# A new written order of all steps, and other engines for 93 of them, in a gated linear attention followed by a gated MLP

## The chip, the core and the metric

The kernel runs on one NeuronCore of a Trainium2 chip. The core has a matrix engine (TensorE, PE), a vector engine (VectorE, DVE), a scalar engine (ScalarE, ACT), a general engine (GpSimd, POOL) and a queue engine (SyncE, SP), each with its own list of instructions that it takes in order, and 16 DMA engines that move data between HBM and on-chip memory. The metric is the device time of one execution in microseconds (us); lower is better.

## What is computed

Two parts follow each other: a linear attention with a complex decay for each key channel, and a gated MLP with a gated residual.

```python
batch, n_heads, seq, head_dim = (4, 8, 768, 48)
mag = np.sqrt(a_re * a_re + a_im * a_im)
scale = np.minimum(mag, 0.999) / (mag + 1e-06)
a_re_n, a_im_n = (a_re * scale, a_im * scale)
for t in range(S):
    new_re = ar * S_re - ai * S_im
    new_im = ar * S_im + ai * S_re
    kv = np.einsum('bhd,bhe->bhde', k[:, :, t], v[:, :, t])
    S_re, S_im = (new_re + kv, new_im)
    y[:, :, t] = np.einsum('bhd,bhde->bhe', q[:, :, t], S_re)
...
g = x @ w_gate                      # x: 3072 x 384, w_gate and w_val: 384 x 1536
gelu = 0.5 * g * (1.0 + erf(g * inv_sqrt2))
val = x @ w_val
ffn_out = gelu * val @ w_out        # w_out: 1536 x 384
res_gate = 1.0 / (1.0 + np.exp(-(x @ w_res)))
return x + res_gate * ffn_out
```

x is the attention's output with the heads side by side: 4 x 768 tokens of 8 x 48 channels.

## The kernel before

**Tiling.** The sequence of each batch is cut into three stretches of 256 tokens. A stretch of a batch is a *pair* p, from 0 to 11: p = 4 s + b for stretch s and batch b. A pair has two *chunks* c of 128 tokens, on the 128 partitions. The recurrence becomes products of triangular matrices inside a chunk and a state of 48 x 48 (twice, for the real and imaginary part) handed from chunk to chunk and, by batch, from pair p to pair p + 4. The MLP works on *units* u of tokens: units 0 to 3 are pairs 0 to 3, units 4 to 7 are two pairs each (4 and 5, 6 and 7, and so on).

**Steps.** Every piece of work is a named step, added with its engine, its function, and what it reads and writes (class Steps, line 354). A step's name is letters, pair (or unit), and then chunk and half. By groups:

- Loads on SP, 192 KB each: Lar, Lai, Lq, Lk, Lvf with pair and chunk (lines 522 to 525 and 889). VC casts v to bf16.
- Gates of a pair (lines 527 to 668): SQI and SQR square the imaginary and real part, ADD adds them, LNR and EXR make the inverse of the magnitude or real part, TH the tangent, LM the logarithm, ATN the angle. CSL and CST are running sums over the tokens (fp32 products with a triangular matrix on PE). EX and EI are exponentials of the sums, in E and Ei. OFF and FR reduce the angle to one turn, ABS its size, SIN and COS the rotation (tile CS).
- State and carries: DR, DS, DI, DT, DE, CDA and CDB are small DMAs on POOL; ML, ME, MM and MN make the decay of the state; CRA and CRB scale a carried row; EN decays the state, EB copies it to bf16, MI and ED add to it.
- Products (lines 691 to 711): QE, KE, QR, KR scale and rotate q and k into padQ and padK. For pairs 0 to 4, TP transposes them on PE and CP evicts; from pair 5 on, QT and KT are transposing DMAs on SP.
- Attention (lines 713 to 808): AT makes scores, AM masks them, DK updates the state, Y makes the output, X casts it to bf16.
- Unit (lines 813 to 882): XT and XC transpose x on PE for pairs 0 to 4, XD is a transposing DMA on SP from pair 5 on. GP and VP are gate and value products, GE the gelu, HM the product of both, RP and SG the residual gate, OP the output product, OT its eviction with the gate, RX adds x, ST stores 192 KB on SP.
- Weights: Wg0 to Wg3 and Wv0 to Wv3 (a quarter each of w_gate and w_val, 288 KB), Wr, Wo0 to Wo2, as casting DMAs on POOL. HOLDW and HOLDO are one-element copies on POOL that read ai of pair 2, chunk 1, and ai of pair 4, chunk 1; POOL goes on when these loads have landed.

**Tables of ACT.** The words log, trig and gelu in the order load the function table for LNR, EXR, LM, EX, EI, ML and ME; for ATN, SIN and COS; and for GE and SG (line 938). Copies, squares and casts run with any.

**What sets the order.** Nothing is reordered at build time: the text ORDER (from line 268) lists all steps, and each engine takes its own steps in that order. The digits after a colon choose the buffers that the step's tiles take. PARAMS['eo'] (from line 64) names the engine of the steps that may go to one of several; without an entry a default holds. A step waits, in its engine's list, for the tiles that it reads and for the release of the buffers that it takes, and everything behind it on that engine waits too. The loop that runs it:

```python
for nm in ORDER(st) if callable(ORDER) else ORDER.split():
    if nm in tables:
        nc.scalar.preload_act_table_set(tables[nm])
    else:
        st.run(*nm.split(":"))
```

Of the kernel before, what the change touches and what calls it, by code (L numbers as in the profile page):

```python
# [79 lines left out]
        'CP4.0.0': 'ACT',  # L80
# [33 lines left out]
        'EN8': 'DVE',  # L114
# [69 lines left out]
        'SQI11': 'DVE',  # L184
        'SQI2': 'DVE',
# [3 lines left out]
        'SQI6': 'ACT',  # L189
# [3 lines left out]
        'SQR0.0': 'ACT',  # L193
        'SQR0.1': 'ACT',
        'SQR1': 'DVE',
        'SQR10': 'ACT',
        'SQR11': 'ACT',
        'SQR2': 'ACT',
# [32 lines left out]
        'X0.1': 'DVE',  # L231
        'X1.0': 'DVE',
        'X1.1': 'DVE',
        'X10.0': 'ACT',
        'X10.1': 'ACT',
        'X11.0': 'DVE',
# [12 lines left out]
        'X7.1': 'DVE',  # L249
        'X8.0': 'ACT',  # L250
        'X8.1': 'ACT',
        'X9.0': 'DVE',
        'X9.1': 'ACT',
        'XC0.0': 'DVE',
        'XC0.1': 'DVE',
        'XC1.0': 'DVE',
        'XC1.1': 'DVE',
        'XC2.0': 'DVE',
        'XC2.1': 'ACT',
        'XC3.0': 'DVE',  # L260
# [23 lines left out]
TH4 VP0.4:1 GE0.5 HM0.3 VP0.0:2 Lai7.1 HM0.4 VP0.1:0 X1.0 trig ATN2 VP0.2:3 HM0.0 XT1.0:11 SIN3:0 HM0.1 VP0.5:2 HM0.2
ATN4 Y1.1:3 CST2.1:0 Lq2.1:2 X1.1 ATN5 CDB0 XC1.0 XT1.1:3 OFF2.1 CST2.0:1 Lq2.0 XC1.1 DR5:1 HM0.5 RP0.0:3 OFF2.0 CDB1
FR2.1 Lq3.1:3 OP0.1.0:2 COS3 FR2.0 DE3:3 Lq3.0 ABS2 SIN2:1 VC2.1 KE2 Lar6.1:2 COS2 OP0.0.0:0 DS5.1:1 Lk3.1:3 OT0.1:0
CRB2 ED1 Lar7.0:1 KR2 GP1.2:1 gelu SG0.0 Lk3.0 GP1.3:2 OT0.0:1 GE1.2 QE2 GP1.0:3 SQI7:3 Lvf3.0:0 GP1.5:0 GE1.0 QR2
VP1.3:1 Lq6.0:1 GE1.5 QE3 TP2.0.1:30 GE1.3 VP1.0:0 CP2.0.1 Lai6.0:1 CSL4.0:211 HM1.3 AT2.0.1:00 log LM5 TP2.0.0:31
# [682 lines left out]
```

## Time and profile before

| | |
|---|---|
| runs | 273.61, 271.89, 273.48 us; median 273.48 |
| profiled execution, its own time | 271.4 us |
| its span, first to last instruction | 269.6 us |
| mean granted clock of TensorE | 0.958 of full |
| DMA | 41.35 MB moved, 153 GB/s in the mean |
| ACT table loads | 32 |

The profile is of one execution. Busy time is the time in which an engine worked at an instruction; a wait in front of an instruction is not busy. A matmul's end is modelled, so PE that shows as busy is not always at its peak rate. In the rows of 40 slices each digit is the busy share of one fortieth of the span in tenths; PEclk is the clock that TensorE was granted, in tenths. In the tables of stretches the columns are named in the head line. The DMA share is the mean busy share of the 16 DMA engines and goes over 1 where packets of several transfers overlap.

### The profile page before, as it was taken

What the parts mean: (1) busy time and instruction counts of PE and PEld (TensorE: products, weight loads), DVE (VectorE), ACT (ScalarE), POOL (GpSimd) and SP (SyncE); (2) the same over time, 40 slices, a digit from 0 to 9 for tenths busy, and PEclk for the clock granted to TensorE, in tenths of its full rate; (3) what the DMA queues carried; (4) which work ended last, traced back from release to release, by engine and by line L of the source; (5) the groups of instructions that cost most, each with busy time, mean ns of one, the idle gap of its engine ahead of it and who ended that gap; (6) DMA issues with size and microseconds to landing.
All of it is one profiled execution on the core that took longest, in us unless ns stands there. A gap on an engine that the chain in (4) does not pass through costs nothing. (4 is left out here: it accounts for less than half of the span.)

```text
span 269.6 us, 5323 instructions
## 1 busy us (share of the span) xinstructions
PE 235.4 (87%) x1926; PEld 147.7 (55%) x1926; DVE 220.9 (82%) x359; ACT 205.3 (76%) x334; POOL 113.6 (42%) x163
## 2 busy tenths in 40 slices
PE   0364778799998989899988999999999999999993
PEld 0121444586775677577844556645556455654451
DVE  0548898999999999999998998978889998733642
ACT  3779999999999999789996899987967843115310
POOL 4003338304436799347695177630853400040001
PEclk9998555999999999999999999999999999999998
DMA  7999999999996999999979969379942484021002
GB/s 147 212 209 210 220 173 186 200 186 191 197 175 139 160 178 166 238 208 174 175 140 229 238 140 183 73 142 244 139 64 72 121 202 123 21 77 65 2 29 88
DMA packets 170714, 41.35 MB, mean 153 GB/s; under 512 B 162624, under 2 KB 170688, under 8 KB 170688
## 3 DMA queue, kind: packets, MB, share of 16 engines
q1 hardware_dynamic: 163200, 37.04, 67.3%
q0 software_dynamic: 7488, 3.97, 11.4%
q8 instruction: 15, 0.25, 0.4%
q14 instruction: 11, 0.09, 0.1%
HBM read 31.33 MB, written 4.76 MB: 134 GB/s over the span
## 5 line engine op out<-in xcount | busy, mean ns | idle before, releaser
L509 ACT ACTIVATE h<-gv 128x512 bf16<-128x512 f32 x72 | 40.0, 598 | 27.4 <-PE gv L837 26.9
L848 DVE SCALAR_TENSOR_TENSOR h<-h,gv 128x512 bf16<-128x512 bf16 x72 | 46.9, 680 | 12.5 <-PE gv L837 8.4
L837 PE MATMUL gv<-xT,wv 128*128 128x256 bf16 (+1 forms) x288 | 54.8, 325 | 1.3 <-DVE ot L867 0.7
L837 PE MATMUL gv<-xT,wg 128*128 128x256 bf16 (+1 forms) x288 | 52.5, 326 | 1.9 <-DVE ot L867 0.7
L862 PE MATMUL sums<-wo,h 128*128 128x384 bf16 x288 | 49.2, 326 | 0.1
L938 ACT ACT_TABLE_LOAD x32 | 41.1, 1283 | 1.3 <-PEq L955 0.7
L874 POOL TENSOR_TENSOR ot<-ot,x 128x384 f32<-128x384 f32 x18 | 19.7, 1101 | 52.6 <-DVE ot L867 47.9
L837 PEld LDWEIGHTS <-wg 128*128 128x128 bf16 x288 | 27.4, 98 | 19.3 <-issue 3.2
L862 PEld LDWEIGHTS <-h 128*128 128x128 bf16 x288 | 27.5, 98 | 17.7 <-issue 0.4
L837 PEld LDWEIGHTS <-wv 128*128 128x128 bf16 x288 | 27.2, 98 | 18.0 <-issue 2.8
L751 DVE TENSOR_TENSOR atm<-at,mask 128x512 bf16<-128x512 f32 x48 | 32.5, 684 | 3.3 <-PE at L748 2.8
L509 ACT ACTIVATE ar<-ar 128x768 f32<-128x768 f32 (+1 forms) x33 | 26.8, 820 | 0.6 <-DVE m L573 0.5
L867 DVE SCALAR_TENSOR_TENSOR ot<-sg,sums 128x384 f32<-128x384 f32 x24 | 13.0, 549 | 11.5 <-PE sums L862 7.3
L631 PE MATMUL sums<-ai,ut 128*128 128x384 f32 x40 | 17.6, 532 | 5.2 <-issue 2.6
L520 POOL CAST v<-vf 128x384 bf16<-128x384 f32 x17 | 13.8, 815 | 17.2 <-DMA vf<-in_v_dram 15.5
L684 POOL DMA_DIRECT2D ai<-G x16 | 14.7, 939 | 14.7 <-ACT ai L509 12.2
L597 PE MATMUL sums<-m,ut 128*128 128x384 f32 x24 | 12.6, 629 | 8.5 <-ACT m L509 8.4
L573 DVE CUSTOM_DVE_ANT_0 m<-m,ar 128x768 f32<-128x768 f32 (+1 forms) x13 | 11.5, 889 | 6.3 <-ACT m L509 6.2
L509 ACT ACTIVATE sg<-sums 128x384 f32<-128x384 f32 x24 | 11.5, 492 | 5.3 <-PE sums L852 5.0
L852 PE MATMUL sums<-wr,xT 128*128 128x384 bf16 x72 | 14.8, 325 | 0.0
L605 POOL DMA_DIRECT2D d<-E x8 | 4.9, 616 | 23.3 <-ACT E L509 23.3
L611 POOL DMA_DIRECT2D m<-d x16 | 13.0, 837 | 3.8 <-DMA d<-Ei 3.7
(94 smaller groups left out, 463.0 us busy)
## 6 DMA issues: line engine op xcount, KB each, us to landing
ar<-in_a_re_dram SPq DMA_DIRECT2D x24, 192.0 KB, 3.8
k<-in_k_dram SPq DMA_DIRECT2D x24, 192.0 KB, 3.9
ai<-in_a_im_dram SPq DMA_DIRECT2D x24, 192.0 KB, 3.8
q<-in_q_dram SPq DMA_DIRECT2D x24, 192.0 KB, 3.7
vf<-in_v_dram SPq DMA_DIRECT2D x24, 192.0 KB, 3.8
out_dram<-ot SPq DMA_DIRECT2D x24, 192.0 KB, 2.0
wv<-in_moe_w_val_dram POOLq DMA_DIRECT2D x4, 288.0 KB, 6.9
wg<-in_moe_w_gate_dram POOLq DMA_DIRECT2D x4, 288.0 KB, 6.8
```

What stands on the lines that cost most here:

```text
L509: return nc.scalar.activation(out=out, in_=in_, func=func, **kw)
L520: return (nc.vector if eng == "DVE" else nc.gpsimd).tensor_copy(out=out, in_=in_)
L611: st.add("DT%d.%d" % (p, u), "POOL", lambda u=u: nc.gpsimd.dma_start(out=st["m3", p][u * D:(u + 1) * D].rearrange("p r h -> p (r h)"), in_ ...
L631: return r + [nc.tensor.matmul(out=o, lhsT=tmat[c if s == 0 else 1], rhs=part(("ai", p), (c,)), start=not both, stop=True)]
L684: st.add("CD%s%d" % (nm, p), "POOL", lambda: nc.gpsimd.dma_start(out=part(("ai", pn), (cn,))[0:1], in_=row[127:128], accum_op=OP.add), r=[ ...
L751: st.add("AM" + sfx, "DVE", lambda: nc.vector.tensor_tensor(out=st["atm", i], in0=st["at", i], in1=mask4, op=OP.mult), r=[("at", i)], w=[( ...
L837: st.add("%sP%d.%d" % (nm.upper(), u, f), "PE", lambda f=f, fs=fs, nm=nm, w=w: [nc.tensor.matmul(out=st[nm + "p", (u, f)][:, j * 256:j * 2 ...
L848: st.add("HM%d.%d" % (u, f), "DVE", lambda f=f, h2=h2: nc.vector.scalar_tensor_tensor(out=h2(), in0=h2(), scalar=0.5, in1=gv(("vp", (u, f) ...
L852: st.add("RP%d.%d" % (u, jj), "PE", lambda jj=jj: [nc.tensor.matmul(out=st["rp", (u, jj)], lhsT=st["xT", u][:, i, jj * 128:(jj + 1) * 128] ...
L862: st.add("OP%d.%d.%d" % (u, jj, hh), "PE", lambda jj=jj, fs=fs: [nc.tensor.matmul(out=st["op", (u, jj)], lhsT=st["h2", u][:, f, jj * 128:( ...
L874: st.add("RX%d.%d" % (u, jj), rese, lambda jj=jj, pc=(p, c), eng=eng: eng.tensor_tensor(out=st["ot", (u, jj)], in0=st["ot", (u, jj)], in1= ...
L938: nc.scalar.preload_act_table_set(tables[nm])
```

## The change

Only PARAMS['eo'] and ORDER differ. The set of steps is the same; the order has 11 log and 10 gelu switches in place of 12 and 11, and 9 trig as before. All buffer counts, units and functions stay.

Engines of 93 steps change. By kind, the number on each engine before and after:

| steps | before | after |
|---|---|---|
| X | ACT 14, DVE 10 | ACT 20, DVE 4 |
| XC | ACT 3, DVE 7 | ACT 4, DVE 6 |
| RX | POOL 18, DVE 6 | POOL 13, DVE 11 |
| SQR | ACT 11, DVE 2 | ACT 8, DVE 5 |
| SQI | ACT 7, DVE 6 | ACT 7, DVE 6 (four swap) |
| VC | ACT 4, DVE 3, POOL 17 | ACT 5, DVE 2, POOL 17 |
| CRA, CRB | ACT 6, DVE 2, POOL 8 | ACT 3, DVE 7, POOL 6 |
| EN, EB, MM, MN | ACT 2, DVE 10, POOL 20 | ACT 2, DVE 6, POOL 24 |
| CP, OFF | ACT 17, DVE 27 | ACT 17, DVE 27 (20 swap) |

Some entries, and the first lines of the order up to the first gate products:

```diff
-        'SQR0.0': 'ACT',
-        'SQR0.1': 'ACT',
+        'SQR0.0': 'DVE',
+        'SQR0.1': 'DVE',
...
-        'SQR2': 'ACT',
+        'SQR2': 'DVE',
...
-        'X0.1': 'DVE',
+        'X0.1': 'ACT',
...
-        'XC0.1': 'DVE',
+        'XC0.1': 'ACT',
...
-Lar0.1:0 Lk0.0:0 Lai0.0:0 Lai0.1 Lai1.1:1 log LNR0.1:0 Lar0.0 SQR0.1 Lai1.0 Lai5.1:2 SQI0.1:0 Lai3.1:3 ADD0.1 LM0.1
-Lar1.0:1 LNR0.0 Lai2.0:4 EXR0.0 CSL0.1:00 SQI1:1 SQI0.0 Lq1.0:0 SQR0.0 EXR0.1 ADD0.0 Lar1.1 TH0.1 TH0.0 Lk0.1 trig
-ATN0.1 ATN0.0 Lar3.1:2 CST0.1:1 Lvf0.0:0 OFF0.1 Lq0.0:1 SQR1 Lai2.1 ADD1 log LM0.0 Lar3.0 CSL0.0:2 FR0.1 LM1 Lar4.1:3
...
-LM3 Lar5.1:1 QE0.0 SQR4 MI0:0 Lq1.1 QR0.0 EX1.1 QR0.1 EI1.1 TP0.0.0:20 Lar5.0 DE1:1 EX1.0 OFF1.0 Wv3 TP0.0.1:31
-Lvf1.0:1 LNR3 FR1.0 Wg2 Lvf2.0:0 CSL3.1:100 ABS1 EXR3 SQI4:0 EI1.0 SQR2 KE1 EI3.1 CP0.0.0 CP0.0.1 AT0.0.0:00 ADD4
-AT0.0.1:11 trig COS1:1 TP0.1.1:00 DK0.1 TH3 TP0.1.0:21 CRB1 DR4:0 SIN1 CSL3.0:3 AM0.0.1 Wv1 ATN3 ADD2 Wg1 KR1 Wg3
-CP0.1.0 Wv2 log LNR2 AM0.0.0 Wg0 CP0.1.1 SQI5:1 Y0.0:0 Wr AT0.1.0:10 EX3.0 CST3.0:2 DS4.1:0 LM2 AM0.1.0 Wo0 QE1 SQR5
...
-OFF3.1 XC0.1 TP1.1.0:20 EX3.1 FR3.1 DS4.0 AT1.0.0:01 LM4 TP1.1.1:31 CRB3 VC1.0 XT0.0:1 EXR2 XC0.0 Lvf2.1:1 CP1.1.1
-GP0.0:0 CP1.1.0 Lai7.0:0 AM1.0.0 Lk2.1:2 GP0.3:1 AM1.0.1 GP0.2:3 ABS3 DK1.0 Y1.0:2 Lk2.0 gelu GE0.3 AT1.1.0:00 MI1:1
...
+Lai0.0:0 Lai1.1:1 Lar0.0:0 Lar0.1 Lar1.0:1 SQI0.0:0 Lar1.1 Lai0.1 log LNR0.0:0 Lai1.0 EXR0.0 SQR0.0 LNR0.1 Lar3.0:2
+EXR0.1 SQR0.1 ADD0.0 Lk0.0:0 TH0.0 LM0.0 SQR1 Lk0.1 CSL0.0:00 SQI0.1 Lar3.1 TH0.1 SQI1:1 Lai3.0:2 trig ATN0.0 ADD1
+ATN0.1 Lai4.0:3 CST0.0:1 ADD0.1 Lai4.1 log LM0.1 Lar4.1:3 LNR1 CSL0.1:2 Lai3.1 OFF0.0 EI0.0 FR0.0 CST0.1:3 Lar2.0:0
...
+KR0.0 Lai5.0:5 ADD3 Lvf0.0:1 KR0.1 log EX1.1 VC0.1:0 OFF1.1 LNR3 Lar5.1:1 Wg0 FR1.1 EX1.0 QE0.0 HOLDO Lai2.1 EXR3
+DE1:1 QR0.0 LM3 Lar5.0 OFF1.0 TP0.0.1:30 QE0.1 EI1.1 SQR2 SQR4 CSL3.1:100 Lk1.0:1 CP0.0.1 ADD4 CRB1 LNR4 QR0.1
+Lvf1.1:0 VC0.0 TP0.1.0:31 EI3.1 FR1.0 EI1.0 Lk1.1 ABS1 AT0.0.1:00 SQI2:0 CP0.1.0 DK0.0 Lvf2.0:1 TP0.0.0:00 EX3.1 MI0:0
+Lq1.0 DE3:2 CP0.0.0 HOLDW AM0.0.1 Lai5.1 AT0.0.0:11 trig COS1:1 VC1.1:1 DK0.1 TH3 DR4:0 CSL3.0:2 Lvf1.0:0 Wv2 AM0.0.0
+ATN3 Wg3 ADD2 Y0.0:0 SIN1 AT0.1.0:00 Wg1 KE1 CST3.0:3 Wv0 KR1 TP0.1.1:10 Wr log EI3.0 CST3.1:0 AM0.1.0 X0.0 Wv3 EXR4
+CP0.1.1 Wv1 OFF3.0 LM2 AT0.1.1:11 Wg2 FR3.0 LNR2 AM0.1.1 Wo2 EX3.0 QE1 CSL2.0:111 Y0.1:1 OFF3.1 XT0.0:30 SQR5 CSL2.1:2
+FR3.1 Wo1 QR1 EX2.1 EXR2 SQI5:1 TP1.0.1:00 LM4 ADD5 EI2.1 DE2:3 X0.1 CP1.0.1 LNR5 XT0.1:2 XC0.0 TP1.0.0:01 ABS3 XC0.1
+Wo0 EXR5 ED0 GP0.5:3 TH2 EX2.0 GP0.0:2 EI2.0 DS4.0:0 CP1.0.0 GP0.1:1 DR5:1 AT1.0.1:00 AT1.0.0:11 CRB3 gelu GE0.1
+AM1.0.1 TP1.1.0:00 GE0.5 AM1.0.0 VP0.0:1 DS4.1 GE0.0 CP1.1.0 GP0.2:3 VC1.0 HM0.0 Lvf2.1:0 TP1.1.1:21 TH5 GE0.2 Lk2.1:2
...
```

Where unit 6 ends and unit 7 begins:

```diff
-DK11.0 HM6.5 GE6.9 VP6.9:3 HM6.10 Y11.0:4 RP6.0:1 HM6.9 AT11.1.1:10 SG6.0 AT11.1.0:01 AM11.1.1 OP6.0.0:2 MI11:1 X11.0
-XD11.0 OP6.2.0:0 OT6.0:0 AM11.1.0 XD10.1 Y11.1:5 OT6.2:1 OP6.1.0:3 X11.1 RX6.2 XD11.1 OP6.3.0:1 ST6.2 OT6.1:2 RX6.1
...
+RP6.3:0 VP6.3:1 HM6.8 SG6.3 RP6.0:0 HM6.3 Y11.0:5 SG6.0 HM6.9 AT11.1.1:10 X11.0 AT11.1.0:01 RP6.1:3 AM11.1.0 XD11.0
+OP6.0.0:1 SG6.1 AM11.1.1 XD10.1 OP6.1.0:0 OT6.0:2 MI11:0 RX6.0 ST6.0 Y11.1:7 OP6.3.0:2 X11.1 XD11.1 OP6.2.0:3 OT6.3:0
```

More of the change, by code (lines that the diff above doesn't have):

```diff
@@ L113 @@
         'EN7': 'POOL',
-        'EN8': 'DVE',
+        'EN8': 'POOL',
         'EN9': 'POOL',
@@ L188 @@
         'SQI5': 'DVE',
-        'SQI6': 'ACT',
+        'SQI6': 'DVE',
         'SQI7': 'ACT',
@@ L204 @@
         'SQR8': 'ACT',
-        'SQR9': 'DVE',
-        'VC0.0': 'ACT',
-        'VC0.1': 'ACT',
+        'SQR9': 'ACT',
+        'VC0.0': 'DVE',
+        'VC0.1': 'POOL',
         'VC1.0': 'POOL',
@@ L284 @@
[L284 to L288, printed above, removed]
```

300 lines of the change are left out of this document (151 added, 149 removed).

## The prediction

> **What bounds the kernel now.** I read the page's busy times and its 40 slices first, then the table of stretches, then the waits of each stretch, the timeline of the first 53 us, and last the groups by shape for the price of each instruction that changes engine.
>
> ```profile
> span 269.6 us, 5323 instructions
> PE 235.4 (87%) x1926; PEld 147.7 (55%) x1926; DVE 220.9 (82%) x359; ACT 205.3 (76%) x334; POOL 113.6 (42%) x163
> PE   0364778799998989899988999999999999999993
> DVE  0548898999999999999998998978889998733642
> ACT  3779999999999999789996899987967843115310
> PEclk9998555999999999999999999999999999999998
> DMA  7999999999996999999979969379942484021002
> ```
>
> ```profile
> core 0: us, PE busy (x) PEld busy (x) DVE busy (x) ACT busy (x) POOL busy (x), PEclk, DMA share, GB/s
> 0.00:25.40 25.40, 9.36 (x14) 3.75 (x14) 10.96 (x23) 18.02 (x29) 6.04 (x17) 1.00 0.98 194
> 25.40:45.80 20.40, 14.29 (x83) 8.63 (x83) 18.25 (x28) 20.27 (x31) 10.47 (x16) 0.50 1.13 192
> 45.80:53.10 7.30, 5.33 (x69) 3.90 (x67) 6.60 (x13) 6.45 (x13) 2.87 (x6) 1.00 1.31 202
> 53.10:142.40 89.30, 84.16 (x861) 63.23 (x861) 87.48 (x140) 84.29 (x133) 54.09 (x74) 1.00 0.97 179
> 142.40:265.40 123.00, 122.28 (x903) 68.15 (x902) 96.48 (x156) 76.29 (x132) 40.09 (x52) 1.00 0.55 119
> 265.40:269.60 4.20, 0.00 (x0) 0.00 (x0) 1.11 (x2) 0.00 (x0) 0.00 (x0) 0.77 0.25 94
> ```
>
> The table splits the run into four parts with different limits. From 142.4 to 265.4 us TensorE (PE) is busy 122.28 of 123.0: nothing but PE work counts there, and the change removes none. The last 4.2 us are the final product's eviction and store. From 53.1 to 142.4, the units 0 to 3, VectorE (DVE) is busy 87.48 of 89.3, ScalarE (ACT) 84.29 and PE 84.16: three engines near full, DVE nearest. Before 53.1, where the first gate product GP0.0 starts, PE is busy 28.98 of 53.1 (9.36 + 14.29 + 5.33), much of it at half clock. There ACT is the full engine: 20.27 of 20.40 us between 25.4 and 45.8, while DVE has 17.3 us idle in the 53.1 (10.96 + 18.25 + 6.60 = 35.8 busy). So an order can win in the first 53 us, where ACT's list decides, win or lose a few us in the middle, and at the end only lose.
>
> ```profile
> ai<-in_a_im_dram SPq DMA_DIRECT2D x24, 192.0 KB, 3.8
> ...
> 0.74 0.45 SPq L525 DMA_DIRECT2D ar<-in_a_re_dram  x1
> 1.87 2.79 SPq L525 DMA_DIRECT2D ai<-in_a_im_dram  x3
> 3.62 0.52 ACT L509 ACTIVATE Ei<-ar 128x384 f32<-128x384 f32 x1 [1.60 <-DMA ar<-in_a_re_dram]
> ...
> 6.55 0.52 ACT L509 ACTIVATE m<-ai 128x384 f32<-128x384 f32 x1 [1.85 <-DMA ai<-in_a_im_dram]
> ...
> 35.27 1.28 ACT L938 ACT_TABLE_LOAD   x1
> ...
> 38.37 0.77 POOL L909 DMA_DIRECT2D wv<-in_moe_w_val_dram  x1
> ...
> 50.45 0.66 POOL L585 DMA_DIRECT2D m<-d  x1 [0.24 <-DMA wg<-in_moe_w_gate_dram]
> ...
> 53.10 2.13 PE L837 MATMUL gv<-xT,wg 128*128 128x256 bf16 x18 [0.45 <-DVE xT L520]
> ```
>
> The first row gives the median us from a load's issue to its landing. The timeline's columns are start, duration, engine, line, operation, tiles, count, and in brackets the idle time before with its releaser. ACT begins when the first load lands (3.62), then waits 1.85 us for the fourth.
>
> **The change part by part.** No step is added or taken out; two of 32 table switches go, and 93 steps change engine. Prices:
>
> ```profile
> L938 ACT ACT_TABLE_LOAD x32 | 41.1, 1283 | 1.3 <-PEq L955 0.7
> L874 POOL TENSOR_TENSOR ot<-ot,x 128x384 f32<-128x384 f32 x18 | 19.7, 1101 | 52.6 <-DVE ot L867 47.9 <-issue 4.4
> L509 ACT ACTIVATE E<-sums 128x384 f32<-128x384 f32 x24 | 11.3, 485 | 0.7 <-PE sums L597 0.6
> L509 ACT ACTIVATE CS<-ai,consts 128x768 bf16<-128x768 f32 x11 | 10.2, 930 | 0.9 <-DVE ai L651 0.7
> L509 ACT ACTIVATE m<-sums,consts 128x384 f32<-128x384 f32 x12 | 6.9, 578 | 2.4 <-PE sums L631 2.2
> L519 ACT CAST x<-y 128x384 bf16<-128x384 f32 x14 | 6.6, 474 | 4.5 <-PE y L799 4.5
> L509 ACT ACTIVATE m<-ai 128x768 f32<-128x768 f32 x5 | 4.2, 834 | 0.0
> L874 DVE TENSOR_TENSOR ot<-ot,x 128x384 f32<-128x384 f32 x6 | 3.4, 571 | 0.1
> L509 ACT ACTIVATE G<-m 32x384 f32<-32x384 f32 x6 | 3.1, 518 | 0.1
> L519 ACT CAST v<-vf 128x384 bf16<-128x384 f32 x4 | 2.0, 504 | 0.0
> L519 ACT COPY xT<-tpx 128x384 bf16<-128x384 bf16 x3 | 1.4, 465 | 0.1
> L509 ACT ACTIVATE m<-ai 128x384 f32<-128x384 f32 x2 | 1.0, 514 | 1.9 <-DMA ai<-in_a_im_dram 1.9
> ```
>
> Each row gives busy us and mean ns of one, then the idle time before.
>
> *Front, to the first gate product.* Both written orders have their first eight table switches here, in the same sequence. I counted the steps of each kind that stand before the first GP (GP0.0 before, GP0.5 after). ACT loses three squares SQR (two halves at 0.514, one whole at 0.834), two v casts VC (0.504 each), two OFF (0.578), one carry row CRB (0.518), and one EX and one EI that move behind (0.485 each): 1.86 + 1.01 + 1.16 + 0.52 + 0.97 = 5.52. It gains one X (0.474), one XC (0.465), and a whole SQI in place of a half one (0.32): 1.26. Net -4.3 us on ACT. DVE takes over the squares, both OFF, the carry row and one cast; even all 5.5 us would find 17.3 us of idle time there. In the new order X0.1 and XC0.1, the last two steps before GP0.5, are on ACT, so ACT's list ahead of them is the path. (Were DVE full, up to those 5.5 us would stand on the path instead.)
>
> The loads are reordered too. ar0.0 comes third, ai0.1 seventh; k0.0 goes from 2nd to 10th, ai5.1 from 8th to 36th, q1.0 from 12th to 35th; ar1, ar3 and ai4, which ACT and DVE need early, come forward. The third load is issued at 1.87 against 0.74, so ACT starts 1.1 us later or more, since loads take 3.8 us in the median and the first took 2.9 (3.62 - 0.74): up to 2.0. The wait of 1.85 at 6.55 goes, because SQI0.0 is on DVE now; what is late next is ai0.1, issued seventh, for which SQI0.1 waits about 1.3 us. Net +0.2 to +1.5; I take +0.9. SP's queue ahead of its 38th item, Lvf2.1, holds the same 37 loads in both, so the bytes to come by then are equal. Front: -4.3 + 0.9 = **-3.4** us, first GP at 49.7. Ends: 0 (DVE or the half-clock PE chain takes ACT's place) and -4.3.
>
> *Middle, units 0 to 3.* ACT gets four more X (1.90), the EX and EI put off (0.97), one COS more (0.93), one state copy EB (about 0.5 by the v cast's row) and one SQI less (0.83): +3.5 on 84.29. DVE's list there comes out level: it loses four X and gains two CP, two CRB, a CRA, an RX. With 87.8 of 89.3 ACT would be as full as DVE, and the two feed each other. Ends: -3 (PE's idle there is 89.3 - 84.16 = 5.1; a better fit removes more than half of it) and +3.5 (every added us waits). I take **+1.0**, nearer to nothing, since the front's lead is partly the same work coming later.
>
> *Late, units 4 to 7.* The two table switches that go (2 x 1.283) are here, and ACT has 123.0 - 76.29 = 46.7 us idle: 0. Residual adds RX move from POOL to DVE (1.101 against 0.571): DVE has 26.5 us idle, and POOL's RX mostly waited: 0. The small state steps EN, MM, MN, EB and the carry rows change between DVE, POOL and ACT, which all have room here: 0. One edge costs: the transfer XD11.1 that lets unit 7 begin now stands behind the store ST6.0 on SP; it stood ahead of all four stores.
>
> ```profile
> L818 SPq DMA_TRANSPOSE xT<-x x14: 1177/1202/2062, 134.0 to 236.8; - x14
> DMA to landing us min/median/max: 2.3/2.6/4.6
> ...
> 239.85 3.40 PE L837 MATMUL gv<-xT,wg 128*128 128x512 bf16 x15
> ```
>
> The last of 14 is issued at 236.8, lands 2.6 us later, and unit 7 starts at 239.85: slack 0.45. Beside a store it may take up to the 4.6 of the slowest: 0 to +1.7, taken +0.3, near the median. The work that hides it is OP6.3 and OP6.2, as two OPs did before.
>
> Sum: -3.4 + 1.0 + 0.3 = **-2.1** us. The profiled execution took 271.4 us, 1.8 outside its span of 269.6; the three runs have a median of 273.48 (271.89 to 273.61), 2.1 above it. A shorter span shifts all of them alike: 273.48 - 2.1 = 271.4 us in the median, 269.3 for a profiled one like this.
>
> **Rivals.**
>
> *The middle takes it back.* ACT's +3.5 is paid in full: -3.4 + 3.5 + 0.3 = +0.4, 273.9 us. For it: ACT and DVE both at 94 to 98% there. Against: DVE, the fuller engine, gets nothing more there.
>
> *Weights land too late (slower).* Wg2 was the second weight issued; it is now the ninth of twelve, behind Wg0, then DE3, the hold on ai2.1, VC1.1 and DR4, then Wv2 Wg3 Wg1 Wv0 Wr Wv3 Wv1. DE3 needs EX3.1, which stands just before the sixth table load (35.27 now; some 34 then, as only part of the lead is there yet), and DE3, the hold and VC1.1 take some 1.6 us of POOL, so Wv2 goes out at about 35.6. Five weights of the old order took from 38.37 to the end of POOL's wait at 50.45: 2.4 us each. Eight then end at 54.8. GP0.3, the first to need Wg2, stands behind six products of 0.71 (2.13 for three) and some 2 us of AT, TP, RP and Y from GP0.5 on: 6.3 us, due at 56.0. Slack 1.2 us, so it decides from 2.55 us a weight. Should these eight go at 3.3 us each, Wg2 lands at 62.0, PE stands 6 us, DK1.0 and Y1.0 too (VC1.0 is behind the seventh weight on POOL): -2.1 + 6.0 = +3.9, 277.4. For it: DMA share 1.13 to 1.31 there, and Wg0 now runs beside loads. Against: loads stop at the same 37th item.
>
> *The clock opens late.* Rows:
>
> ```profile
> 21.90:25.30 3.40, 0.86 (x3) 0.30 (x2) 3.37 (x7) 3.37 (x6) 1.93 (x2) 1.00 1.10 219
> 35.00:40.00 5.00, 3.85 (x34) 3.26 (x34) 5.00 (x8) 4.94 (x7) 2.16 (x4) 0.50 1.22 192
> ```
>
> The clock fell at 25.4, after a stretch with PE busy 0.86 of 3.4 us, and half clock held to 45.8 though PE was busy 70% (14.29 of 20.40), 77% in the second row. If the new order's PE work opens it only some 5 us into the unit's stream, at 55, half of the PE work between 45.8 and 55 comes on top: (3.9 x 0.73 + 5.3) / 2 = 4.1, with 0.73 the busy share of 45.8 to 53.1. -2.1 + 4.1 = +2.0, 275.5. Against: PE's list before the first GP holds the same kinds of bursts.
>
> The Trainium skill, "TensorE: Matmul & The Clock Gate", section "What's actually happening", says that the gate closes after an idle stretch of about 3.4 us and opens after as much sustained work. The first row agrees with the closing; by the second, "sustained" must mean close to full, so by that rule too the opening could wait for the unit's stream.
>
> *The middle tightens as well.* PE's 5.1 us of idle fall to 2: -3.4 - 3.0 + 0.3 = -6.1, 267.4. For it: loads that DVE needs between 60 and 80 us stand no later on SP than before. Against: DVE at 98%.
>
> **How the numbers follow.** Chances: forecast 0.50, middle takes it back 0.18, weights late 0.14, clock late 0.06, middle tightens 0.12. The forecast's own range is -4.3 to 0 us (269.2 to 273.5). One per cent is 2.7 us, about what a measurement of this kernel tells from no change; the limits are 270.7 and 276.2. Faster: 0.23 of the forecast's 0.50 and 0.12: 0.35. Slower: weights 0.14, and 0.08 from the bad ends of the middle and the clock: 0.22. The rest, 0.43, is within. The range 267.4 to 277.0 leaves out some 0.07 below and 0.1 above.
>
> **What would show it.** A first gate product at about 49.7, with ACT over 95% busy from 25 us on, shows the front right; if ACT waits there, the order lacks something that I took as ready. PE's gv, or POOL, waiting for a weight's DMA between 50 and 62 shows the weights; a granted clock of 0.50 beyond 46 shows the clock. With DVE and ACT both above 95% busy and PE idle about 5 us in the units 0 to 3, the middle is as forecast. PE idle by over 2 us in the last 125 us, above all ahead of unit 7, would mean that the late part isn't covered, and would make the prediction wrong, as would a first gate product later than 52.

## The result and the profile after

| | before | after |
|---|---|---|
| median of 21 runs each | 271.89 us | 269.06 us |
| ratio after / before, 95% interval | | 0.9889 [0.9866, 0.9912] |
| profiled execution, its span | 269.6 us | 266.8 us |
| its mean granted clock | 0.958 | 0.966 |
| ACT table loads | 32 | 30 |

The changed kernel is faster by 1.1%, some 3.0 us of 271.9 (2.4 to 3.6); the profiled spans differ by 2.8. Four slow runs of the changed kernel (271.3 to 272.0 us, mean clock 0.959 to 0.960) are left out of the ratio; the other 17 took 266.0 to 270.0 us. First the page of the changed kernel (busy times, and the rows of 40 slices), then its table of stretches.

```profile
span 266.8 us, 5303 instructions
...
PE 236.3 (89%) x1913; PEld 149.0 (56%) x1926; DVE 221.0 (83%) x360; ACT 203.0 (76%) x334; POOL 105.2 (39%) x160
...
PE   0475786989999997998999999999999999999993
...
DVE  1849999689999999999899999898988889643723
ACT  3899799979999997999898899988658862225310
...
PEclk9999559799999999999999999999999999999999
```

```profile
core 0: us, PE busy (x) PEld busy (x) DVE busy (x) ACT busy (x) POOL busy (x), PEclk, DMA share, GB/s
0.00:21.20 21.20, 9.08 (x13) 3.70 (x14) 11.36 (x25) 15.16 (x23) 4.01 (x15) 1.00 0.93 183
21.20:45.00 23.80, 17.28 (x116) 10.78 (x114) 23.02 (x38) 22.30 (x35) 11.15 (x18) 0.71 1.11 196
45.00:47.65 2.65, 1.09 (x13) 0.89 (x12) 2.53 (x6) 2.57 (x6) 0.63 (x2) 0.93 1.31 199
47.65:136.60 88.95, 83.80 (x871) 63.76 (x869) 82.70 (x132) 82.54 (x134) 47.21 (x68) 0.98 0.99 179
136.60:262.50 125.90, 125.08 (x908) 69.85 (x919) 100.32 (x162) 80.47 (x140) 42.22 (x60) 1.00 0.60 128
262.50:266.80 4.30, 0.00 (x0) 0.00 (x0) 1.11 (x2) 0.00 (x0) 0.00 (x0) 0.88 0.15 55
```

The late stretch is as full of PE work as it was (125.08 of 125.90). The cut at 136.60 lies inside the output products of unit 3, the one at 142.40 in the table of before inside unit 4, so the lengths of the middle and the late stretch are not compared one by one. What is new lies ahead of 47.65, where the first gate product now starts, against 53.10. Before, DVE was busy 18.25 of the 20.40 us from 25.40 on (89%); now it is busy 23.02 of the 23.80 us from 21.20 on (97%). Timeline rows of the changed kernel (start, duration, engine, line, operation, tiles; in brackets the idle time before and its releaser):

```profile
5.75 0.52 ACT L509 ACTIVATE Ei<-ar 128x384 f32<-128x384 f32 x1 [3.73 <-DMA ar<-in_a_re_dram]
...
8.74 0.52 ACT L509 ACTIVATE m<-m 128x384 f32<-128x384 f32 x1 [0.94 <-DVE m L573]
...
32.76 0.84 ACT L509 ACTIVATE m<-ai 128x768 f32<-128x768 f32 x1 [1.28 <-DMA ai<-in_a_im_dram]
...
47.65 3.59 PE L837 MATMUL gv<-xT,wg 128*128 128x256 bf16 x18
...
50.01 1.28 ACT L938 ACT_TABLE_LOAD   x1
```

The last row is the load of the gelu table, ahead of which no gelu can run; in before it was this row:

```profile
54.02 1.28 ACT L938 ACT_TABLE_LOAD   x1
```

The first gate products lead by 5.4 us, but ACT, which must take them, leads by 4.0. That 4.0 is the better mark of the front. How ACT got there can be counted: its busy time and idle time up to that load. One stretch and the sum line of each table, first before, then after (the sum's length is the time of the gelu load):

```profile
10.70:25.40 14.70, 7.74 (x12) 3.25 (x12) 8.49 (x14) 12.36 (x19) 2.71 (x3) 1.00 1.07 211
...
sum 54.02, PE 29.89 PEld 17.11 DVE 36.70 ACT 45.64 POOL 19.38; mean PE 7.47 PEld 4.28 DVE 9.17 ACT 11.41 POOL 4.84
```

```profile
10.06:24.68 14.62, 10.79 (x16) 4.03 (x14) 10.77 (x18) 14.30 (x22) 0.68 (x1) 1.00 1.03 200
...
sum 50.01, PE 29.82 PEld 17.00 DVE 38.27 ACT 42.38 POOL 16.97; mean PE 7.46 PEld 4.25 DVE 9.57 ACT 10.60 POOL 4.24
```

ACT's work fell by 3.3 us (45.64 to 42.38) and its idle time by 0.8 (8.38 to 7.63). Read that way the prediction's account, work off ACT's list, looks confirmed. The experiments say otherwise.

### The profile page after: what moved, and what is told of

The parts are those of the page before. It is cut to its first block, busy times and chain, and to the rows that moved or that the text cites. A ratio compares the mean times of both kernels' runs of the same rounds, so it can differ in the third digit from the quotient of the medians.

```text
span 266.8 us, 5303 instructions
## 1 busy us (share of the span) xinstructions
PE 236.3 (89%) x1913; PEld 149.0 (56%) x1926; DVE 221.0 (83%) x360; ACT 203.0 (76%) x334; POOL 105.2 (39%) x160
## 4 chain that ended last, share of the span: by engine, by line
PE 58%; DVE 12%; DMA 9%; ACT 8%; issue 4%; SPq 3%; POOL 3%; DVEq 0%; ACTq 0%; POOLq 0%
PE gv L837 25%; PE sums L862 17%; DMA wv<-in_moe_w_val_dram 4%; PE sums L631 4%; SPq L525 3%; PE sums L852 3%; ACT L938 3%; PE sums L597 3%; PE at L748 3%; DMA KT<-padK 2%; DVE h L848 2%; DMA ai<-in_a_im_dram 1%; DMA vf<-in_v_dram 1%; PE y L796 1%; ACT m L509 1%
## 5 line engine op out<-in xcount | busy, mean ns | idle before, releaser
L509 ACT ACTIVATE h<-gv 128x512 bf16<-128x512 f32 x72 | 40.7, 599 | 24.7 <-PE gv L837 24.0
L848 DVE SCALAR_TENSOR_TENSOR h<-h,gv 128x512 bf16<-128x512 bf16 x72 | 47.3, 681 | 11.0 <-PE gv L837 10.0
L837 PE MATMUL gv<-xT,wg 128*128 128x256 bf16 (+1 forms) x281 | 54.5, 331 | 0.8 <-DVE qk L520 0.3
L862 PE MATMUL sums<-wo,h 128*128 128x384 bf16 x288 | 49.7, 326 | 0.0
L874 POOL TENSOR_TENSOR ot<-ot,x 128x384 f32<-128x384 f32 x13 | 15.1, 1162 | 49.3 <-DVE ot L867 49.2
L509 ACT ACTIVATE ar<-ar 128x768 f32<-128x768 f32 x30 | 25.0, 843 | 0.7 <-DVE m L573 0.3
L597 PE MATMUL sums<-m,lt 128*128 128x384 f32 x24 | 12.4, 604 | 9.6 <-ACT m L509 9.6
L684 POOL DMA_DIRECT2D ai<-G x16 | 13.5, 861 | 13.2 <-ACT ai L509 6.6
L520 POOL CAST v<-vf 128x384 bf16<-128x384 f32 x17 | 11.1, 654 | 18.4 <-DMA vf<-in_v_dram 18.3
L509 ACT ACTIVATE m<-m 96x8 f32<-96x8 f32 (+2 forms) x29 | 13.2, 468 | 2.4 <-DMA d<-m 1.3
L608 POOL DMA_DIRECT2D d<-Ei x8 | 4.5, 556 | 24.9 <-ACT Ei L509 24.8
L736 PE MATMUL tp<-ident,padQ 128*96 128x128 bf16 x80 | 8.8, 239 | 5.9 <-POOL HOLDO L901 3.5
```

Source lines behind the costliest of these rows:

```text
L509: return nc.scalar.activation(out=out, in_=in_, func=func, **kw)
L597: st.add("CSL%d.%d" % (p, c), "PE", lambda c=c: nc.tensor.matmul(out=st["csl", (p, c)], lhsT=lmat[c], rhs=part(("m2", p), (c,)), start=Tru ...
L684: st.add("CD%s%d" % (nm, p), "POOL", lambda: nc.gpsimd.dma_start(out=part(("ai", pn), (cn,))[0:1], in_=row[127:128], accum_op=OP.add), r=[ ...
L837: st.add("%sP%d.%d" % (nm.upper(), u, f), "PE", lambda f=f, fs=fs, nm=nm, w=w: [nc.tensor.matmul(out=st[nm + "p", (u, f)][:, j * 256:j * 2 ...
L848: st.add("HM%d.%d" % (u, f), "DVE", lambda f=f, h2=h2: nc.vector.scalar_tensor_tensor(out=h2(), in0=h2(), scalar=0.5, in1=gv(("vp", (u, f) ...
L862: st.add("OP%d.%d.%d" % (u, jj, hh), "PE", lambda jj=jj, fs=fs: [nc.tensor.matmul(out=st["op", (u, jj)], lhsT=st["h2", u][:, f, jj * 128:( ...
```

## The experiments

Every kernel was timed beside runs of before on the same chip; the ratio is to those. One chip had e1, e2, e3 and e8, another e4 to e7, a third e9 to e11, a fourth e12; runs of kernels on one chip can also be set beside each other. The table gathers what the readings need; "rest" is the span less the time of the gelu load.

| run | gelu load, us | span | rest | median, us | ratio [95%] |
|---|---|---|---|---|---|
| before | 54.02 | 269.6 | 215.6 | | 1 |
| after | 50.01 | 266.8 | 216.8 | 269.06 | 0.9889 [0.9866, 0.9912] |
| e1_engines_only | 55.81 | 279.8 | 224.0 | 281.85 | 1.0388 [1.0338, 1.0438] |
| e2_order_only | 51.36 | 281.9 | 230.5 | 284.48 | 1.0478 [1.0436, 1.0521] |
| e3_act_back | 51.00 | 267.3 | 216.3 | 269.07 | 0.9914 [0.9880, 0.9948] |
| e4_vc_early | 50.01 | 265.5 | 215.5 | 267.38 | 0.9870 [0.9824, 0.9916] |
| e5_fill_clock | 49.16 | 263.5 | 214.3 | 265.85 | 0.9828 [0.9790, 0.9867] |
| e6_x_back | 49.75 | 267.4 | 217.7 | 269.37 | 0.9931 [0.9900, 0.9962] |
| e7_ar_first | 49.71 | 265.2 | 215.5 | 266.91 | 0.9862 [0.9828, 0.9896] |
| e8_x_early | 49.78 | 265.7 | 215.9 | 267.19 | 0.9837 [0.9801, 0.9872] |
| e9_before_fill | 53.03 | 269.3 | 216.3 | 271.65 | 1.0009 [0.9982, 1.0036] |
| e10_wg2_late | 49.77 | 265.4 | 215.6 | 267.29 | 0.9855 [0.9818, 0.9892] |
| e11_joined | 49.10 | 264.1 | 215.0 | 268.28 | 0.9874 [0.9829, 0.9919] |
| e12_fill_gp | 50.00 | 265.7 | 215.7 | 266.51 | 0.9811 [0.9777, 0.9844] |

Runs of one kernel spread by up to 4 us (after: 266.0 to 270.0), so a profile is one draw, and ratios that differ by 0.3% are read as no difference.

### Order or engines

Theory A is the prediction's: ACT's list sets the front, and work that leaves it is the lead. Theory B is that the order makes it. e1 and e2 split the change in its two halves.

```diff
 e1_engines_only: ORDER of before,  PARAMS['eo'] of after
 e2_order_only:   ORDER of after,   PARAMS['eo'] of before
```

> The written order of before, with the engines of after for all 93 steps. Theory A (the lead comes from the 4.3 us of work that leaves ACT's list in the front): the table load for gelu, which stands at 54.02 us in before and 50.01 in after, comes at 50 to 52 here, and the kernel is faster than before, ratio 0.989 to 0.997. Theory B (the order makes the lead, the engines only suit it): the gelu load stays at 53.5 or later, since work lands on engines that the old order gave no room, and the ratio is 1.003 or more.

> The written order of after, with the engines of before. Theory A: ACT has its 4.3 us back in the front, the gelu load comes at 53 to 54.5 us, and the lead is gone: ratio 0.997 to 1.010. Theory B: the gelu load comes by 51.5 us, ratio 0.988 to 0.995.

The engines alone make the gelu load later by 1.8 us, the order alone makes it earlier by 2.7 (54.02 to 51.36), though ACT then does as much work ahead of it as in before (45.67 us against 45.64). In the front that is theory B. B's open limit for e1 (1.003 or more) holds too, but neither theory foresaw that the end would be 3.9% and 4.8% slower than before. A row of each table, of e2 and then of after, for the same 50 us of the middle:

```profile
100.00:150.00 50.00, 43.18 (x435) 32.39 (x434) 45.78 (x69) 41.03 (x66) 29.69 (x43) 0.97 0.77 146
```

```profile
100.00:150.00 50.00, 46.57 (x447) 32.37 (x448) 48.28 (x77) 43.98 (x75) 28.86 (x43) 1.00 0.96 179
```

With the engines of the other order PE loses 3.4 us of work in 50, and DVE and ACT are both less busy. Among the waits in this stretch of e2 are one of PE for DVE's h (3.5 us) and one of ACT for DVE's ai (3.1); where the rest of the loss arises was not followed up. Neither half has an effect of its own that could be added to the other's. The split says what the front owes to the order; it says nothing of the rest.

e3 stays in after's order and puts back on ACT eight steps of the front alone.

```diff
-        'SQR0.0': 'DVE',  'SQR0.1': 'DVE',  'SQR2': 'DVE',
-        'OFF0.1': 'DVE',  'OFF1.0': 'DVE',  'OFF1.1': 'DVE',
-        'VC0.0': 'DVE',   'CRB1': 'DVE',
+        (the same eight)  'ACT'
```

> After, with eight steps of the front put back on ACT: SQR0.0, SQR0.1, SQR2, OFF0.1, OFF1.0, OFF1.1, VC0.0 and CRB1, 4.6 us of ACT work by the rows of before. Theory A (ACT's list is the path to the first gelu): the waits that ACT has there in after (1.28 for ai, 0.94 and 0.26 early) take up at most 1.5 of it, the gelu load moves from 50.0 to 53.1 or later, and the end is later than after's by 2 to 4.6 us, ratio to before 0.996 to 1.006. Theory B (the chain through PE at half clock is the path, ACT's fullness only follows): the gelu load comes by 51.5 and the ratio is at most 0.993.

```profile
9.50:24.58 15.08, 10.25 (x16) 3.73 (x14) 10.58 (x17) 14.77 (x22) 1.43 (x3) 1.00 1.10 214
...
sum 51.00, PE 28.04 PEld 15.72 DVE 34.60 ACT 46.04 POOL 18.21; mean PE 7.01 PEld 3.93 DVE 8.65 ACT 11.51 POOL 4.55
```

This is e3's table as above: ACT has 46.04 us of work ahead of the gelu load, more than the 45.64 of before, and still gets there at 51.00. Its idle time is 4.96 us, against 8.38 in before, and only 0.9 of it comes after the first load has landed: here ACT's list is the path, as theory A says. So of the 4.0 us of lead, 3.0 stay with ACT's work restored: they are waits of ACT that the new order has filled. The stretch with the second to the fifth table load shows the largest part: 2.34 us idle in before (14.70 - 12.36), 0.31 here (15.08 - 14.77). The eight moved steps, 4.6 us by their rows and 3.7 of ACT's busy time (46.04 - 42.38, since neighbouring rows of ACT overlap by some 0.1), brought 1.0. Why so little? With the steps gone, ACT finds other waits in place of the work. In after they are 0.94 for DVE's sum and 1.28 for ai (above). In e8, and much the same in e6, e7 and e10, all of which have after's front, they are these, from the timeline of e8:

```profile
8.52 0.52 ACT L509 ACTIVATE m<-m 128x384 f32<-128x384 f32 x1 [0.94 <-DVE m L573]
...
29.62 0.84 ACT L509 ACTIVATE ar<-ar 128x768 f32<-128x768 f32 x1 [0.33 <-DVE m L573]
...
35.64 0.84 ACT L509 ACTIVATE ai<-ai 128x768 f32<-128x768 f32 x1 [1.06 <-DVE ai L554]
```

The last of them is ATN3, which waits for TH3, multiplied late by DVE. ACT waits 2.33 us for DVE in e8, and in e3 for DVE not once that its table of waits shows. The work that left ACT went to DVE, and DVE is then nearly as full as ACT was. The gelu load fell within B's limit (51.5 or earlier; A had 53.1 or later), though the expectation of e3 gave B another reason, the chain through PE at half clock, which e5 below doesn't bear out. At the end the loss of e3 beside after, 0.0025 in the ratio, is within the intervals. Beside e8, on the same chip, it is larger: all six runs of e3 (268.9 to 269.5) lie above all six of e8 (266.2 to 267.5), 1.9 us between the medians. So at the end the eight steps may be worth up to 2 us; with them on ACT the kernel still is 0.9% under before.

### Does the first gate product set the pace?

```diff
- ... Y0.1:1 OFF3.1 XT0.0:30 SQR5 CSL2.1:2 FR3.1 Wo1 QR1 EX2.1 EXR2 SQI5:1 TP1.0.1:00 LM4 ADD5 EI2.1 DE2:3 X0.1
- CP1.0.1 LNR5 XT0.1:2 XC0.0 TP1.0.0:01 ABS3 XC0.1 Wo0 EXR5 ED0 GP0.5:3
+ ... Y0.1:1 OFF3.1 X0.1 XT0.0:30 SQR5 CSL2.1:2 FR3.1 XC0.0 XT0.1:3 Wo1 QR1 EX2.1 XC0.1 EXR2 SQI5:1 TP1.0.1:00
+ GP0.5:3 LM4 ADD5 EI2.1 DE2:3 CP1.0.1 LNR5 TP1.0.0:01 ABS3 Wo0 EXR5 ED0
```

> After, with X0.1, XT0.1, XC0.0, XC0.1 and GP0.5 moved up in the order: X0.1 waited 3 us behind other ACT work in after though its y was ready at 42.7. No ACT work is saved. Theory A (ACT's work up to the gelu load sets the pace): the first gate product comes at 44.5 to 46 instead of 47.65, but the gelu load stays at 49.5 to 50.2 and the end gains at most 0.8 us: ratio 0.986 to 0.990. Theory B (the first gate product's time sets the end): the end gains 2 us or more, ratio 0.982 or less.

The first gate product came at 44.95, 2.7 us earlier than after's, and the gelu load at 49.78: 0.2 earlier, as theory A has it. The ratio, 0.9837, lies between the two expectations and its interval overlaps after's. The profile sides with A: its rest of 215.9 is near that of e4, e7 and e10 (215.5 to 215.6), whose first gate product came no earlier than 47.3. PE's early product only fills a PSUM bank until ACT loads the gelu table.

### The loads

```diff
-Lai0.0:0 Lai1.1:1 Lar0.0:0 Lar0.1 ...
+Lar0.0:0 Lai0.0:0 Lai1.1:1 Lar0.1 ...
```

> After, with one load moved: ar0.0 is issued first, as a load of ar was in before, ahead of ai0.0 and ai1.1. ACT then starts at 4.0 to 4.7 us instead of 5.75. The prediction's load term (+0.9 for the late start) says that the gelu load comes 0.7 to 1.0 earlier, at 49.0 to 49.3, and the end likewise, ratio 0.985 to 0.987. The rival (what ACT does first waits again behind it, for ADD0.0's sum and for ai0.1) says that ACT's waits of 0.94 and 0.26 us behind it grow by as much, and the gelu load stays at 49.8 to 50.1, ratio 0.988 to 0.990.

The timeline of ACT in e7:

```profile
3.61 0.52 ACT L509 ACTIVATE Ei<-ar 128x384 f32<-128x384 f32 x1 [1.59 <-DMA ar<-in_a_re_dram]
...
6.47 0.52 ACT L509 ACTIVATE Ei<-ar 128x384 f32<-128x384 f32 x1 [1.79 <-DMA ar<-in_a_re_dram]
...
8.49 0.52 ACT L509 ACTIVATE m<-m 128x384 f32<-128x384 f32 x1 [0.94 <-DVE m L573]
```

ACT starts 2.1 us earlier than in after, waits 1.79 us more for the second half of ar, waits the same 0.94 for the sum, and loads gelu at 49.71, where e6, e8 and e10, without this edit, load it at 49.75 to 49.78. In the profile the rival holds: the late start cost nothing. The ratio, 0.9862, lies in the other band (0.985 to 0.987), but so does that of e10 (0.9855), which leaves the loads as they are in after, so it doesn't decide.

### The middle: X on ACT

```diff
-        'X1.0': 'ACT', 'X1.1': 'ACT', 'X3.0': 'ACT', 'X4.0': 'ACT', 'X4.1': 'ACT',
+        'X1.0': 'DVE', 'X1.1': 'DVE', 'X3.0': 'DVE', 'X4.0': 'DVE', 'X4.1': 'DVE',
```

> After, with the five casts X1.0, X1.1, X3.0, X4.0 and X4.1 of the middle put back from ACT to DVE: 2.4 us less on ACT, some 2 more on DVE. The prediction's middle term (ACT gets 3.5 us of work there and 1.0 of it is paid) says that the end is 0.5 to 1.0 us earlier than after's, ratio 0.985 to 0.987. The rival (DVE is the fuller engine or PE waits for DVE's products) says 1 to 2 us later, ratio 0.992 to 0.997. No change within 0.2 per cent would say that neither list is the path there.

0.9931, in the rival's band: casts on DVE are worse. The interval touches after's, but on the same chip the median of e6 is 2.0 to 2.5 us above those of e4 and e7, which have the casts on ACT. The profile has the gelu load in its place (49.75) and a rest of 217.7, some 2 us over the others. Its waits of PE between 118 and 140 us are one:

```profile
PE at L748 <- DMA KT<-padK: 2.1, 1, 2.1
```

The scores of pair 5 wait for the transposing DMA of its k, which DVE feeds; in after this wait was 1.2, in e4, e7, e8 and e10 0.7 to 0.9. So this wait accounts for 1.2 to 1.4 of the 2 us. Putting X on ACT relieved the fuller engine.

### The weights

Times of after: POOL's row of the first of eight weights, a small DMA that stands behind the weights and waited for one, its row of VC1.0, and the landing of the eighth weight, Wg2, issued at 41.99; then PE's Y1.0 and GP0.3.

```profile
36.66 0.80 POOL L909 DMA_DIRECT2D wv<-in_moe_w_val_dram  x1
...
51.94 0.52 POOL L582 DMA_DIRECT2D d<-m  x1 [1.07 <-DMA wv<-in_moe_w_val_dram]
...
54.55 0.54 POOL L520 CAST v<-vf 128x384 bf16<-128x384 f32 x1
```

```profile
DMA to landing us min/median/max: 12.3/12.3/12.3
```

```profile
55.15 0.36 PE L796 MATMUL y<-v,atm 128*128 128x48 bf16 x8 [0.76 <-POOL v L520]
...
56.23 0.82 PE L837 MATMUL gv<-xT,wg 128*128 128x256 bf16 x6
```

Wg2 landed at 54.3 (41.99 + 12.3), 2.2 us a weight from 36.66, and GP0.3 ran at 56.23: no wait of PE for a weight. But VC1.0, behind the weights on POOL, made PE stand 0.76. Two runs work at this.

```diff
 e4_vc_early:   VC1.0 from behind DS4.1 to ahead of Wo1
 e10_wg2_late:  Wg2 from behind Wv1 to behind Wo1
```

> After, with the cast VC1.0 moved up on POOL from behind DS4.0, DR5 and DS4.1 to ahead of Wo1, so that it no longer stands behind the waits for weights. Its ratio is to be set beside after's 0.9889. If the wait that the weights cause there is on the path: the 0.8 us that PE stands in front of Y1.0 goes, the load Lvf2.1 goes out at 44 to 48 us instead of 55.1, and the end is 0.5 to 1.0 us earlier than after's, ratio 0.985 to 0.987. If the middle is set by other engines: the wait goes and the end stays, ratio 0.988 to 0.990.

> After, with the quarter Wg2 moved back by two more weights, behind Wo1. In after it was the ninth weight issued, landed at 54.3 us, 2.2 us for each of the eight since 36.7, and GP0.3 that needs it ran at 56.2. Two weights more put the landing at 58.5 to 59.5. The prediction's rival (a late weight stands PE, and the end pays): PE waits 2 to 3 us for wg at GP0.3 and the end is later than after's by 1.5 to 3 us, ratio 0.995 to 1.000. If PE's wait there is covered (ACT and DVE full), the ratio is at most 0.992.

e4: the wait went, Lvf2.1 was issued at 42.3 instead of 55.1, and the ratio is 0.9870, with after inside its interval. But in e6, e8 and e10 the wait was gone as well, without that edit: their POOL lists reached the weights at 34.2 to 34.7 us, some 2 earlier than in after. In after's profiled run the queue of loads ran late: the load behind the 1.28 for ai went out at 27.11, in e8 at 25.00 and in e10 at 25.20. So what e4 is worth is not settled: it may guard against a late load, and shows no gain when none is late. e10 did not test what it was meant to: Wg2, two places later, was issued at 41.66 and landed 13.0 later, at 54.7, only 0.4 later than in after. Whether a later weight would stand PE was not seen. As a kernel that changed nothing on the path, e10's 0.9855 shows how far a ratio can lie from after's 0.9889 by chance.

### The clock

Stretches of 3.41 us of the changed kernel, cut where the granted clock steps (the column behind POOL's):

```profile
23.38:26.79 3.41, 0.28 (x1) 0.00 (x0) 3.34 (x7) 3.40 (x5) 1.37 (x3) 1.00 1.02 203
...
30.20:33.62 3.42, 2.73 (x28) 2.52 (x28) 3.04 (x7) 2.14 (x5) 0.00 (x0) 0.50 1.12 219
...
37.03:40.44 3.41, 3.41 (x20) 2.30 (x16) 3.30 (x5) 3.38 (x5) 3.41 (x5) 0.50 0.98 154
40.44:43.86 3.42, 2.87 (x29) 1.52 (x27) 3.38 (x7) 3.42 (x7) 3.12 (x5) 1.00 1.29 197
43.86:47.27 3.41, 1.25 (x16) 1.01 (x17) 3.29 (x6) 3.33 (x7) 0.74 (x1) 1.00 1.32 203
47.27:50.68 3.41, 3.41 (x22) 2.48 (x20) 1.75 (x3) 3.39 (x6) 1.77 (x3) 0.50 1.31 202
```

Half clock lasted 17.1 us (13.65 from 26.8, 3.41 from 47.3) against 20.48 before. Could the shorter half clock be the lead, or the clock's second fall a loss? Extra products fill PE's gaps: FZ is n fp32 products of 128 x 128 into a free PSUM bank that nobody reads.

```diff
...
+    st.add("FZ%d" % i, "PE", lambda i=i, n=n: [nc.tensor.matmul(
+        out=st["fz%d" % i, 0][:, 0:128], lhsT=tmat[1], rhs=tmat[1], start=True, stop=True) for _ in range(n)],
+        w=[("fz%d" % i, 0)])
 e5_fill_clock:  after,  behind CST1.1 (n 8), CSL3.1, TP0.1.0, TP0.0.0 (2 each), AT0.0.0 (1), CST3.1 (2), TP1.0.1 (3)
 e9_before_fill: before, behind CSL1.0 (10), CST1.1 (5), CST1.0 (9), TP0.0.1 (2), CSL3.1 (8), TP0.1.0 (2), CSL3.0 (6)
 e12_fill_gp:    after,  behind TP1.0.1 (6)
```

> After, with 20 extra fp32 products of 128 x 128 in PE's gaps between 23 and 46 us, into PSUM banks that are free there and that nobody reads: they only keep PE busy, about 0.4 us each at full clock. Theory A (ACT's list sets the front): the granted clock stays at 1.0 over most of 27 to 47 us, and the gelu load moves from 50.0 by less than 0.8 us; the first gate products run at full clock, so the end gains up to 1.5 us, ratio 0.983 to 0.990. Theory B (the chain through PE at half clock sets the front): the gelu load comes by 48.5 and the end gains 2 us or more, ratio 0.981 or less. If an extra product stands in the way of a step that others wait for, the ratio is over 0.991.

> Before, with 42 extra fp32 products of 128 x 128 in PE's gaps between 22 and 42 us, into the PSUM bank of y, which is free there. The run of after with such products moved its gelu load from 50.0 to 49.2 us. If the lead of after's order were mainly the shorter stretch of half clock (17.1 us against 20.5), the gelu load of before, at 54.02, would come here by 51.5 and the ratio be 0.990 or less. If the two lists of ACT and DVE set the front in before as well, the gelu load moves by less than 1.2 us, to 52.8 or later, and the ratio is 0.993 to 1.001.

> After, with 6 extra fp32 products of 128 x 128 (some 1.3 us) in the one gap of PE behind TP1.0.1, ahead of the first gate products. In after the granted clock fell to 0.50 over these (3.59 us for 18 products, 2.32 in e5). If e5's gain beside after came from the gate products at full clock, the gelu load stays at 49.7 to 50.1, the 18 products take 2.1 to 2.4 us, and the ratio is 0.982 to 0.986. If it came from the whole front at full clock, which moved the gelu load by 0.6 to 0.9 us, the ratio stays at 0.987 to 0.990.

In e5 the clock was 1.0 but for one stretch of 3.4 us, and the gelu load came at 49.16: some 0.6 earlier than in e6, e7, e8 and e10, 0.85 earlier than in after. In e9 PE had the full clock, and the gelu load of before came 1.0 us earlier, at 53.03; the end gained nothing (1.0009). So half clock costs the front of either kernel about a microsecond at most, and the lead of 4.0 is not made of it: with the clock near full in both, e9 and e5 still lie 3.9 apart (53.03 and 49.16). e12 aims at the second fall alone. The gate products then ran at full clock, but look at what comes next, in PE's timeline:

```profile
47.65 2.32 PE L837 MATMUL gv<-xT,wg 128*128 128x256 bf16 x18
...
51.95 0.81 PE L837 MATMUL gv<-xT,wv 128*128 128x256 bf16 x6 [1.06 <-ACT h L509]
```

PE saved 1.3 us on the 18 products (3.59 to 2.32) and stood 1.06 ahead of VP0.0, which began at 51.95, in after at 51.98: gelu, not PE's clock, decides. The runs of after say the same: in eight of the 17 the clock's mean is 0.965 to 0.968, in nine 0.971 to 0.974, about one such stretch more or less, and both groups took 268.6 us in the mean. The runs of before that the ratios of e1 to e12 rest on don't: 30 with a mean clock of 0.953 to 0.962 took 272.0 us in the mean, 13 with 0.971 to 0.975 took 270.5. A late run may have lost clock, or lost time by the clock; e9, at full clock, took 271.7, so the clock alone doesn't bring the 1.5 us. And e12's ratio, 0.9811, is the lowest of all and its interval lies below after's, as e5's nearly does. Its profile, which is of its slowest run (267.5 of 265.6 to 267.5), has less PE work left behind the gelu load than e4, e8 and e10 (206.0 us against 206.8 to 207.0), but so much more idle time that its rest is the same, 215.7. No path is seen by which the extra products would shorten the run; this stays open.

e11 joins e4, e5, e7 and e8 (FZ of e5 with n 14, 3, 2, 2, 1, 2, the last, 4, behind GP0.5 in place of TP1.0.1).

> After, with the moves of e4 (VC1.0 early), e7 (ar0.0 first) and e8 (X0.1, XT0.1, XC and GP0.5 early) and extra products in PE's gaps as in e5, placed for this order. If these gains add up (0.2, 0.3, 0.5 and 0.6 per cent by the ratios so far), the ratio is 0.973 to 0.979; if they are one and the same gain, since each only brings forward the same first stretch of PE work, it stays at 0.981 to 0.985, the best of them.

0.9874: the sum doesn't add up, and not even the best single one remains, though its one profile (264.1) looked like it; that run was the fastest of its six (265.9 to 269.3). The fastest version measured is e12, 1.9% under before (1.6 to 2.2).

## Why the prediction held, step by step

- **The forecast.** A change of -2.1 us was foretold; the ratio makes it -3.0 (2.4 to 3.6). The measured gain stands on the limit between "faster by over 1%" and "within 1%", which had 0.35 and 0.43. That the size came so near is luck: two errors in the front, of opposite sign, nearly cancelled.
- **Front, -3.4, first gate product at 49.7.** The size was near (4.0 at the gelu load; the product itself at 47.65), the account was not. The failed step is "Net -4.3 us on ACT ... ACT's list ahead of them is the path", with DVE's "17.3 us of idle time" as cover. ACT's busy time up to the gelu load fell by 3.3 and not 4.3, as its rows overlap; and e3 shows that eight moved steps of 4.6 us by their rows bring only 1.0 at the gelu load: between 21 and 45 us DVE is full to 97%, and ACT, busy 22.30 of 23.80 there and not the over 95% that the prediction named as its sign, waits for DVE or a load. DVE's 17.3 us were counted over the whole front; 14.4 of them lay before 25.4 us. The prediction names a full DVE in brackets and as the end of its range at 0, but adds nothing for it to its sum.
- **Load reorder, +0.9.** ACT did start 2.1 us later, but the profile of e7 shows that it cost 0 at the gelu load, because the next waits take it up. And the order, to which the prediction gave only this loss, gave about 3.0 of the 4.0, by filling ACT's waits, above all between 10 and 25 us. The term of -4.3 was really about -1.0 and that of +0.9 about 0; the -3.0 of the order stood nowhere in the sum.
- **Middle, +1.0.** After's profile gives back 1.2 (rest 216.8 against 215.6): PE has 1.0 more work left behind the gelu load (206.5 against 205.5) and 0.2 more idle time. In e4, e7, e8, e10 and e12 the rest is 215.5 to 215.9, as in before. The 3.0 of the ratio is also 1.0 short of the 4.0 of the front, where e4, e7, e8 and e10 gained 3.5 to 4.4 at the end by their ratios. So the size may be right for after itself; whether it loses this as a rule or by the late loads of its one profile stays open. The reason given (ACT's +3.5) has the wrong sign by e6 as far as the casts X go: on ACT they relieve DVE. DVE and ACT were forecast above 95%; both were at 93% (82.70 and 82.54 of 88.95), with PE idle 5.15, as forecast.
- **Late, +0.3.** Not paid: PE 125.08 of 125.90, no wait of PE from 137 us on in the table of waits, none ahead of unit 7. The rest of the late part was 0, as foretold.
- **Rivals.** "Weights land too late" came nearest: Wg2 landed at 54.3 (54.8 was worked out), 2.2 us each, below the 2.55 from which it decides; its side branch, VC1.0 behind the weights, did cost PE 0.76 us in the profile. "The clock opens late": it opened at 40.4 and fell again at 47.3, over the first gate products, which cost nothing since gelu wasn't there yet. The two rivals of the middle: neither.

## What to carry to other kernels

When work moves between two engines, count the idle time of the taker in the stretch where the work will run, not over the whole phase; here, with both at 93 to 98%, work taken from one came back as a wait for the other. An order and its choice of engines are one design: each half alone cost 4 to 5% here. And mark a stage by the instruction that nothing can pass (here the table load for gelu): the first product led by 5.4 us and in e8 by 8.2, while the load led by 4.0 and 4.2, and the end gained 3.0 (2.4 to 3.6) and, by e8's ratio, 4.4 (3.5 to 5.4).

## What the runs showed of the hardware

In these traces the granted clock steps on a grid of 3.41 us, as if each stretch decided for the next. By the rows above, at full clock a stretch with PE busy 0.28 or 1.25 of 3.41 us was followed by half clock, one with 2.87 was not; at half clock 2.73 did not open it, nor 2.85 in before, and only the stretch that was busy 3.41 of 3.41 did. The row of before:

```profile
35.59:39.00 3.41, 2.85 (x31) 2.60 (x31) 3.41 (x6) 3.37 (x5) 1.16 (x2) 0.50 1.27 197
```

The Trainium skill, "TensorE: Matmul & The Clock Gate", section "What's actually happening", has the gate close after an idle window of about 3.4 us and open after a busy one of that length. The length agrees; but a window need not be idle to close it (0.86 of 3.40 busy in the row of the prediction, 1.25 of 3.41 here), and busy meant nearly or wholly so. One caution: the stretch with 1.25 held only transposes on PE (TP and XT), those with 2.73 and 2.85 many of them, and no run here shows whether a transpose counts like another product. What this is worth must be asked of the engine that comes next: removing nearly all half clock moved the gelu load by 0.6 to 1.0 us.
